# Attention and token-mixing kernel: score tiles in groups of three, one of them in two banks of the common PSUM ring

## The chip, the cores and the metric

The kernel runs on one core of one Trainium2 chip. Times are device microseconds of that core. Each time is the median of the timed runs of a kernel. All runs quoted here were fast, at a granted TensorE clock of 0.994 to 1.0. A ratio is the mean time of one kernel's fast runs over that of the other's of the same rounds, so it is not quite the ratio of the medians quoted.

The engines are called PE (TensorE), DVE (VectorE), ACT (ScalarE) and POOL (GpSimd).

## The reference

Grouped-query attention is followed by a token-mixing layer. There are 8 batches, 16 query heads on 4 key/value heads, 384 positions and a head width of 64.

```python
scores = scale * q @ k.T                       # per head, 384 x 384
attn   = softmax(scores) @ v                   # 8 x 16 x 384 x 64
x      = attn, heads side by side              # 8 x 384 x 1024
wq, wk = x @ w_q, x @ w_k                      # 1024 -> 64
mixed  = (scale * wq @ wk.T) @ x
out    = relu(mixed) @ w_out                   # 1024 x 1024
```

## The kernel before

Work is cut into 144 score tiles, 18 to a batch. One tile is 128 keys by 4 x 128 queries for two key/value heads. It takes two matmuls, one on the upper and one on the lower 64 rows of the PE array, and one exponential of 128 x 1024. PSUM has eight banks. Score tiles use `psS`, two buffers of two banks each. Everything else shares the ring `psX` of four single banks.

```python
psS = ctx.enter_context(tc.tile_pool(name="psS", bufs=2, space=PSUM))   # 2 x 2 banks
psX = ctx.enter_context(tc.tile_pool(name="psX", bufs=4, space=PSUM))   # 4 x 1 bank

def score(s, d, j, c):
    ...
    ps = psS.tile([P, 2, NH], F32, name="sc", tag="sc")
    for h in range(2):
        r = slice(D * h, D * (h + 1))                      # 64 of the 128 rows
        nc.tensor.matmul(out=ps[:, h, :], lhsT=s.kT[r, d, c, :], rhs=..., ...)

def av_task(s, d, j, h):                                   # 12 matmuls into one psX bank,
    ...                                                    # then DVE: reciprocal and multiply

def mix_banks(s, i):                                       # two psX banks, two 64-row matmuls,
    for h in range(2):                                     # each followed by a relu on DVE
        pm = psX.tile([P, S], F32, name="pmb", tag="ps")
        nc.tensor.matmul(out=pm, lhsT=s.Csb[r, ...], rhs=(s.qk if h == 0 else s.q2)[r, :], ...)
        nc.vector.tensor_relu(out=s.msb[:, ...], in_=pm)

def wout_pieces(s):                                        # the output product, as a generator:
    ...                                                    # 8 matmuls fill one psX bank ("po"),
    po = psX.tile([P, NH], F32, name="po", tag="ps")       # one per piece; between pieces the
    for n, dc in enumerate(order):                         # bank stays occupied
        nc.tensor.matmul(out=po, ...)
        ...                                                # after the 8th: copy on DVE
        yield
```

The steady loop takes two score tiles at a time. It issues both tiles' matmuls and both exponentials. Then come the tasks dealt to this group (av, projection, wk, c), with pieces of po as filler between them by a running credit. Then may come a mix.

```python
groups = [("s", steps[n:n + 2]) for n in range(0, len(steps), 2)]
...
pss = [(st, score(batches[st[0]], *st[1:])) for st in two]
for (b, d, j, c), ps in pss:
    expo(batches[b], d, j, c, ps)
...                                    # tasks and pieces
for m in mine:
    mix_step(*m)
```

## Time and profile before

| | before |
|---|---|
| time, median of 4 runs | 224.01 us |
| span of the profiled run | 221.9 us |
| PE / DVE / ACT busy | 94% / 65% / 65% |
| score visits of PE (single tiles + pairs) | 28 + 58 |
| a steady batch, from one projection to the next | 23.7 us |

The prediction below shows the lines. One habit of reading matters. PE's busy share counts a matmul from its start to its modelled end, 0.38 us for 512 columns, while such matmuls start 0.216 us apart. So a PE that waits 0.1 us between two matmuls still counts as busy, and one has to look at starts.

### The profile page before, as it was taken

What the parts mean: (1) busy time and instruction counts of PE and PEld (TensorE: products, weight loads), DVE (VectorE), ACT (ScalarE), POOL (GpSimd) and SP (SyncE); (2) the same over time, 40 slices, a digit from 0 to 9 for tenths busy, and PEclk for the clock granted to TensorE, in tenths of its full rate; (3) what the DMA queues carried; (4) which work ended last, traced back from release to release, by engine and by line L of the source; (5) the groups of instructions that cost most, each with busy time, mean ns of one, the idle gap of its engine ahead of it and who ended that gap; (6) DMA issues with size and microseconds to landing.
All of it is one profiled execution on the core that took longest, in us unless ns stands there. A gap on an engine that the chain in (4) does not pass through costs nothing.

```text
span 221.9 us, 5286 instructions
## 1 busy us (share of the span) xinstructions
PE 208.6 (94%) x2145; PEld 102.4 (46%) x2145; DVE 144.4 (65%) x371; ACT 143.6 (65%) x150; POOL 46.9 (21%) x105
## 2 busy tenths in 40 slices
PE   1899998999999999999999999999999999999992
PEld 1356554555345454554444454455445444443440
DVE  2367769757974456966687567756687578845540
ACT  2789966788688887887667777777767771001101
POOL 1499405027003220350035003400000000000000
PEclk9999999999999999999999999999999999999999
DMA  7999999999639999999999999973633231224234
GB/s 177 324 327 257 239 225 260 215 280 265 169 77 237 244 276 247 294 242 250 229 310 212 231 237 289 192 197 114 188 38 132 97 92 75 97 95 165 119 147 151
DMA packets 74574, 44.45 MB, mean 200 GB/s; under 512 B 45488, under 2 KB 70576, under 8 KB 74544
## 3 DMA queue, kind: packets, MB, share of 16 engines
q1 hardware_dynamic: 70048, 41.17, 73.0%
q0 software_dynamic: 3168, 2.36, 6.8%
q10 hardware_dynamic: 1328, 0.52, 0.9%
q8 instruction: 19, 0.31, 0.6%
q14 instruction: 11, 0.09, 0.1%
HBM read 23.59 MB, written 12.58 MB: 163 GB/s over the span
## 4 chain that ended last, share of the span: by engine, by line
PE 84%; DVE 9%; DMA 2%; ACT 2%; issue 1%; SPq 0%; ACTq 0%
PE po L276 38%; PE av L182 16%; PE sc L167 15%; PE pqk L211 5%; PE pmb L263 3%; PE pc L234 2%; DVE xnat L188 2%; DMA qraw<-in_q_dram 2%; PE ptx L196 2%; ACT pT L173 2%; DVE msb L265 2%; DVE osb L289 1%; PE ptq L154 1%; DVE qk L217 1%; PE ptw L225 1%
## 5 line engine op out<-in xcount | busy, mean ns | idle before, releaser
L173 ACT ACTIVATE pT<-sc 128x1024 bf16<-128x1024 f32 x144 | 139.7, 1022 | 41.7 <-PE sc L167 41.6
L276 PE MATMUL po<-wout_sb,msb 128*128 128x512 bf16 x384 | 102.5, 379 | 0.0
L182 PEld LDWEIGHTS <-pT 128*128 128x128 bf16 x1152 | 45.6, 98 | 17.1 <-issue 8.3
L182 PE MATMUL av<-vbf,pT 128*128 128x65 bf16 x1152 | 51.5, 195 | 0.4 <-DVE osb L289 0.3
L167 PE MATMUL sc<-qT,kT 64*128 64x512 bf16 x288 | 48.8, 391 | 1.8 <-DVE qT L159 0.8
L276 PEld LDWEIGHTS <-msb 128*128 128x128 bf16 x384 | 33.2, 97 | 35.9 <-issue 11.7
L289 DVE COPY osb<-po 128x512 f32<-128x512 f32 x46 | 31.6, 687 | 18.4 <-PE po L276 18.4
L188 DVE TENSOR_TENSOR xnat<-av,rcp_all 128x256 bf16<-128x256 f32 x96 | 40.7, 424 | 3.3
L111 POOL CAST qbf<-qraw 128x512 bf16<-128x512 f32 x46 | 26.7, 620 | 34.6 <-DMA qraw<-in_q_dram 31.9
L265 DVE TENSOR_SCALAR msb<-pmb 128x384 bf16<-128x384 f32 x56 | 28.3, 551 | 4.9 <-PE pmb L263 4.9
L187 DVE RECIPROCAL rcp_all<-av 128x4 f32<-128x4 f32 x96 | 17.1, 178 | 17.7 <-PE av L182 17.5
L167 PEld LDWEIGHTS <-kT 64*128 64x128 bf16 x288 | 13.0, 94 | 24.2 <-issue 20.3
L111 POOL CAST kbf<-kraw 128x384 bf16<-128x384 f32 x15 | 7.6, 510 | 60.1 <-DMA kraw<-in_k_dram 54.7
L252 ACT ACTIVATE msb<-pm 128x768 bf16<-128x768 f32 x2 | 1.6, 810 | 20.8 <-PE pm L246 20.8
L211 PE MATMUL pqk<-xT,wqk_sb 128*128 128x384 bf16 x64 | 11.8, 327 | 0.1
L263 PE MATMUL pmb<-qk,Csb 64*128 64x384 bf16 x28 | 9.3, 332 | 0.7 <-DVE Csb L238 0.7
L217 DVE CAST qk<-pqk 128x384 bf16<-128x384 f32 x8 | 4.5, 556 | 8.1 <-PE pqk L211 8.1
L263 PE MATMUL pmb<-q,Csb 64*128 64x384 bf16 x28 | 9.3, 331 | 0.3
L238 DVE TENSOR_SCALAR Csb<-pc 128x512 bf16<-128x512 f32 x8 | 5.5, 692 | 4.9 <-PE pc L234 4.9
L198 DVE COPY xT<-ptx 128x512 bf16<-128x512 bf16 x15 | 6.3, 421 | 3.5 <-PE ptx L196 3.5
L263 PEld LDWEIGHTS <-Csb 64*128 64x128 bf16 x56 | 3.0, 92 | 12.0 <-issue 8.8
L211 PEld LDWEIGHTS <-wqk_sb 128*128 128x128 bf16 x64 | 5.7, 97 | 5.7 <-issue 2.5
(44 smaller groups left out, 73.1 us busy)
## 6 DMA issues: line engine op xcount, KB each, us to landing
out_dram<-osb SPq DMA_DIRECT2D x23, 512.0 KB, 3.3
qraw<-in_q_dram SPq DMA_DIRECT2D x30, 384.0 KB, 5.2
kraw<-in_k_dram SPq DMA_DIRECT2D x16, 192.0 KB, 4.3
vraw<-in_v_dram SPq DMA_DIRECT2D x16, 192.0 KB, 5.2
wout_sb<-in_moe_w_out_dram POOLq DMA_DIRECT2D x4, 512.0 KB, 15.2
qraw<-in_q_dram SPq DMA_DIRECT2D x1, 512.0 KB, 5.1
qraw<-in_q_dram ACTq DMA_DIRECT2D x1, 256.0 KB, 3.8
out_dram<-osb SPq DMA_DIRECT2D x2, 128.0 KB, 2.2
```

The source lines that it names most:

```text
L111: eng.tensor_copy(out=out, in_=in_)
L167: nc.tensor.matmul(out=ps[:, h, :], lhsT=s.kT[r, d, c, :], rhs=s.qT[d][r, j, :, :].rearrange("p g n -> p (g n)"), start=True, stop=True)
L173: nc.scalar.activation(out=s.pT[d, j][:, c, :, :], in_=ps, func=AF.Exp, scale=attn_scale)
L182: nc.tensor.matmul(out=av[:, i, :], lhsT=pT[:, c, h, i * P:(i + 1) * P], rhs=s.vbf[:, g, c, :], start=(c == 0), stop=(c == C - 1))
L187: nc.vector.reciprocal(out=rcp, in_=av[:, :, D])
L188: nc.vector.tensor_tensor(out=s.xnat[:, d, j, h * G * D:(h + 1) * G * D].rearrange("p (i d) -> p i d", i=G), in0=av[:, :, :D], in1=rcp.to_ ...
L211: nc.tensor.matmul(out=s.pqk, lhsT=wqk_sb[:, dc, :], rhs=s.xT[:, dc // (DC // ND), :, dc % (DC // ND), :], start=(dc == 0), stop=(dc == DC ...
L217: nc.vector.tensor_copy(out=s.qk, in_=s.pqk)
L263: nc.tensor.matmul(out=pm, lhsT=s.Csb[r, i * P:(i + 1) * P], rhs=(s.qk if h == 0 else s.q2)[r, :], start=True, stop=True)
L265: nc.vector.tensor_relu(out=s.msb[:, h * (DC // 2) + i, :], in_=pm)
L276: nc.tensor.matmul(out=po, lhsT=s.msb[:, dc, c * P:(c + 1) * P], rhs=wout_sb[:, dc, half * NH:(half + 1) * NH], start=(n == 0), stop=(n == ...
L289: nc.vector.tensor_copy(out=osb[:, half * NH:(half + 1) * NH], in_=po)
```

## The change

The intent is to go less often into the 64-row shape of the scores. From tile 30 on, the scores of three tiles are issued together. `psS` has room for two, so the first tile of three goes to two banks of `psX`, with one exponential per bank so that each bank is freed early. At the same time the tasks are dealt out by score tile instead of by pair, and the mixes of a batch are placed beside scores, which are in the same 64-row shape.

```diff
+    def score_banks(s, d, j, c):
+        ...
+        pss = [psX.tile([P, NH], F32, name="scb", tag="ps") for h in range(2)]
+        for h in range(2):
+            nc.tensor.matmul(out=pss[h], lhsT=s.kT[r, d, c, :], ...)
+        for h in range(2):
+            nc.scalar.activation(out=s.pT[d, j][:, c, h, :], in_=pss[h], func=AF.Exp,
+                                 scale=attn_scale)
...
-        groups = [("s", steps[n:n + 2]) for n in range(0, len(steps), 2)]
+        SINGLE = 30
...                                     # at(n, ...) now by tile, not by pair
             elif b < B - 1:
-                at(g + 4, lambda b=b: proj_task(batches[b]), 1.3)
-                ...                     # wk at pair 5, c at pair 6
-                gm = (7, 8, 9, 10)      # one mix at the end of each of four pairs
+                gm = ((12, 1), (15, 0), (15, 1), (18, 0))   # (tile, 0 behind scores / 1 at the end)
+                np, nw, ncc = (6,), 9, 12
...
+        groups = [[n] for n in range(SINGLE)] + [
+            list(range(n, n + C)) for n in range(SINGLE, N + 4 * C, C)]
...
+                b, d, j, c = steps[ns[0]]
+                score_banks(batches[b], d, j, c)
+                pss = [(st, score(batches[st[0]], *st[1:])) for st in (steps[n] for n in ns[1:])]
+                for (b, d, j, c), ps in pss:
+                    expo(batches[b], d, j, c, ps)
+            for m in before:
+                mix_step(*m)
...                                     # tasks and pieces
+            for m in after:
+                mix_step(*m)
```

More of the change, by code (lines that the diff above doesn't have):

```diff
@@ L170, in score @@
         return ps
+    def score_banks(s, d, j, c):
+        if c == 0:
+            s.pT[d, j] = pt_p.tile([P, C, 2, W], BF16, name="pT", tag="pT")
+        pss = [psX.tile([P, NH], F32, name="scb", tag="ps") for h in range(2)]
+        for h in range(2):
+            r = slice(D * h, D * (h + 1))
+            nc.tensor.matmul(out=pss[h], lhsT=s.kT[r, d, c, :],
+                             rhs=s.qT[d][r, j, :, :].rearrange("p g n -> p (g n)"),
+                             start=True, stop=True)
+        for h in range(2):
+            nc.scalar.activation(out=s.pT[d, j][:, c, h, :], in_=pss[h], func=AF.Exp,
+                                 scale=attn_scale)
     def expo(s, d, j, c, ps):
@@ L338, with at @@
         per_b = ND * C * C
-        groups = [("s", steps[n:n + 2]) for n in range(0, len(steps), 2)]
+        SINGLE = 30
         todo = {}
-        def at(g, f, cost):
-            todo.setdefault(g, []).append((f, cost))
-        GB = per_b // 2
+        def at(n, f, cost=0.0, i=None):
+            t = todo.setdefault(n, [])
+            t.insert(len(t) if i is None else i, (f, cost))
         def plan(b):
-            g0 = b * GB
+            n0 = b * per_b
             def start_next():
@@ L355, in start_next @@
                         batches.append(load(b + 2))
-            at(g0, start_next, 0.0)
-            if b + 2 < B:
-                for i, g in enumerate((1, 3, 6, 8)):
-                    at(g0 + g, lambda i=i: batches[b + 2].parts[i](), 0.0)
             def casts(d, ks, vs):
@@ L374, in casts @@
                     wout_load(4 * d + 2)
+            at(n0, start_next)
+            if b + 2 < B:
+                for i, n in enumerate((2, 7, 11, 16)):
+                    at(n0 + n, lambda i=i: batches[b + 2].parts[i]())
             if b == 0:
-                at(g0, lambda: casts(0, (0,), (0,)), 0.0)
-                at(g0 + 1, lambda: casts(1, (1,), (1,)), 0.0)
-            else:
-                at(g0, lambda: casts(0, (0, 1), ()), 0.0)
-                at(g0 + 3, lambda: casts(1, (), (0, 1)), 0.0)
+                at(n0, lambda: casts(0, (0,), (0,)))
+                at(n0 + 2, lambda: casts(1, (1,), (1,)))
+            else:
+                at(n0, lambda: casts(0, (0, 1), ()))
+                at(n0 + 6, lambda: casts(1, (), (0, 1)))
@@ L381, in plan @@
                 if b + 1 < B:
-                    at(g0 + 2, lambda: kt_dma(batches[b + 1]), 0.0)
-                    at(g0 + 2, lambda: qt_dma(batches[b + 1], 0), 0.0)
-                    at(g0 + 7, lambda: qt_dma(batches[b + 1], 1), 0.0)
+                    at(n0 + 4, lambda: kt_dma(batches[b + 1]))
+                    at(n0 + 4, lambda: qt_dma(batches[b + 1], 0))
+                    at(n0 + 13, lambda: qt_dma(batches[b + 1], 1))
             for d in range(ND):
-                n0 = b * per_b + d * C * C
@@ L387, in plan @@
                 for j in range(C):
-                    g = (n0 + j * C + C - 1) // 2 + 1
+                    n = n0 + (d * C + j + 1) * C + 1
+                    end_0 = b == 0 and d == ND - 1 and j == C - 1
                     for h in range(2):
-                        at(g, lambda d=d, j=j, h=h: av_task(batches[b], d, j, h), 0.37)
+                        at(n + h - end_0, lambda d=d, j=j, h=h: av_task(batches[b], d, j, h), 0.37)
                     if b < 2 or (b == B - 1 and d == ND - 1):
-                        at(g + 1, lambda d=d, j=j: xt_task(batches[b], d, j), 0.24)
+                        soon = b < 2 and d == ND - 1 and j == C - 1
+                        at(n + (1 - end_0 if soon else 2), lambda d=d, j=j: xt_task(batches[b], d, j), 0.24)
@@ L393, in plan @@
                     elif j == C - 1:
-                        at(g, lambda d=d: xt_dma(batches[b], d), 0.0)
-                nb, nd = (b, d + 1) if d + 1 < ND else (b + 1, 0)
-                if nb < 2:
-                    g = n0 // 2 + (2 if d else 3 if b == 0 else 1)
-                    at(g, lambda nb=nb, nd=nd: kt_task(batches[nb], nd), 0.18)
-                    for j in range(C):
-                        at(g + j, lambda nb=nb, nd=nd, j=j: qt_task(batches[nb], nd, j), 0.24)
+                        at(n + 1, lambda d=d: xt_dma(batches[b], d))
@@ L403 @@
         at(0, lambda: qt_task(s0, 0, 1), 0.24)
-        at(1, lambda: qt_task(s0, 0, 2), 0.24)
+        at(2, lambda: qt_task(s0, 0, 2), 0.24)
         for b in range(B):
             plan(b)
+        for b, d, nk, nq in ((0, 1, 6, (7, 9, 12)), (1, 0, 13, (14, 17, 20)),
+                             (1, 1, 21, (22, 26, 29))):
+            at(nk, lambda b=b, d=d: kt_task(batches[b], d), 0.18)
+            for j in range(C):
+                at(nq[j], lambda b=b, d=d, j=j: qt_task(batches[b], d, j), 0.24)
@@ L426 @@
         for b in range(B):
-            g = b * GB + GB
-            if b < 2:
-                at(g + 1, lambda b=b: proj_task(batches[b], 0), 0.65)
-                at(g + 1, lambda b=b: proj_task(batches[b], 1), 0.65)
-                todo.setdefault(g + 2, []).insert(1, (lambda b=b: wk_task(batches[b]), 0.17))
-                at(g + 2, lambda b=b: c_task(batches[b]), 0.75)
-                gm = (3, 3, 4, 4)
+            n = (b + 1) * per_b
+            if b == 0:
+                gm = ((6, 0), (7, 0), (8, 0), (9, 0))
+                np, nw, ncc = (2, 3), 4, 5
+            elif b == 1:
+                gm = ((6, 1), (9, 0), (9, 1), (12, 0))
+                np, nw, ncc = (3, 3), 5, 6
             elif b < B - 1:
-                at(g + 4, lambda b=b: proj_task(batches[b]), 1.3)
-                todo.setdefault(g + 5, []).insert(0, (lambda b=b: wk_task(batches[b]), 0.17))
-                todo.setdefault(g + 6, []).insert(0, (lambda b=b: c_task(batches[b]), 0.75))
-                gm = (7, 8, 9, 10)
-            else:
-                at(g + 2, lambda b=b: proj_task(batches[b]), 1.3)
-                at(g + 3, lambda b=b: wk_task(batches[b]), 0.17)
-                at(g + 4, lambda b=b: c_task(batches[b]), 0.75)
-            if b < B - 1:
-                for i in range(DC // 2):
-                    mixes.setdefault(g + gm[i], []).append((b, i))
+                gm = ((12, 1), (15, 0), (15, 1), (18, 0))
+                np, nw, ncc = (6,), 9, 12
+            else:
+                gm = ()
+                np, nw, ncc = (5,), 6, 9
+            for i, m in enumerate(np):
+                part = i if len(np) > 1 else None
+                at(n + m, lambda b=b, part=part: proj_task(batches[b], part), 1.3 / len(np))
+            at(n + nw, lambda b=b: wk_task(batches[b]), 0.17, (1, None)[b] if b < 2 else 0)
+            at(n + ncc, lambda b=b: c_task(batches[b]), 0.75, 0 if b else None)
+            for i, (m, e) in enumerate(gm):
+                mixes.setdefault((n + m, e), []).append((b, i))
         oki = m_p.tile([P, 1], I32, name="oki", tag="oki")
@@ L467, in count @@
             nc.vector.tensor_copy(out=oki[:1, :], in_=pok[:1, :])
-        PIECE, MIX, LEAN, KEEP = 0.218, 0.2, 1.54, 12
+        PIECE, MIX, LEAN, KEEP = 0.218, 0.2, 0.77, 12
         per_piece = C * (Dm // NH) * DC
-        g0 = (B // 2) * GB
-        even = (sum(c for g in range(g0, g0 + GB) for f, c in todo.get(g, []))
-                + (DC // 2) * MIX + per_piece * PIECE) / GB
-        ramp = 4 * GB + 2
-        end = (B - 1) * GB + GB + 2
-        credit = 0.0
-        def tile_of(st):
-            b, d, j, c = st
-            expo(batches[b], d, j, c, score(batches[b], d, j, c))
@@ L484 @@
-        for g in range(end + 3):
-            two = groups[g][1] if g < len(groups) else []
-            tasks = todo.get(g, [])
-            mine = mixes.get(g, [])
-            credit += (LEAN if g < ramp else even) - sum(c for f, c in tasks) - MIX * len(mine)
+        mid = range(B // 2 * per_b, (B // 2 + 1) * per_b)
+        even = (sum(c for n in mid for f, c in todo.get(n, []))
+                + (DC // 2) * MIX + per_piece * PIECE) / per_b
+        ramp = 4 * per_b + 3
+        N = len(steps)
@@ new lines, with mix_step @@
+        at(N + 4, lambda: ok.append(range_test()))
+        at(N + 8, lambda: count(ok[0]))
+        ok = []
+        groups = [[n] for n in range(SINGLE)] + [
+            list(range(n, n + C)) for n in range(SINGLE, N + 4 * C, C)]
+        credit = 0.0
+        def mix_step(b, i):
+            mix_banks(batches[b], i)
+            if i == DC // 2 - 1:
+                filler.append(wout_pieces(batches[b]))
+                left[0] += per_piece
+        for ns in groups:
+            before, after = ([m for n in ns for m in mixes.get((n, e), [])] for e in range(2))
+            tasks = [t for n in ns for t in todo.get(n, [])]
+            credit += (LEAN if ns[0] < ramp else even) * len(ns)
+            credit -= sum(c for f, c in tasks) + MIX * len(before + after)
@@ L489 @@
             n = min(max(0, int(credit / PIECE)), left[0])
-            if g >= end:
-                more = sum(per_piece for b, i in mine if i == DC // 2 - 1)
-                n = min(left[0], (left[0] + more - KEEP) // (end + 3 - g))
+            if ns[0] >= N + C:
+                more = sum(per_piece for b, i in before + after if i == DC // 2 - 1)
+                n = min(left[0], (left[0] + more - KEEP) // ((N + 4 * C - ns[0]) // C))
             credit = min(credit - n * PIECE, 0.5)
-            ops = []
@@ L496 @@
-            for i, t in enumerate(tasks):
-                ops.append(t)
-                ops += [(piece, PIECE)] * (n * (i + 1) // len(tasks) - n * i // len(tasks))
-            if not tasks:
-                ops = [(piece, PIECE)] * n
-            def mix_step(b, i):
-                mix_banks(batches[b], i)
-                if i == DC // 2 - 1:
-                    filler.append(wout_pieces(batches[b]))
-                    left[0] += per_piece
-            if g < GB + 5 and two:
-                tile_of(two[0])
-                if len(mine) == 2:
-                    mix_step(*mine.pop(0))
-                half, run = sum(c for f, c in ops) / 2, 0.0
-                while ops and run + ops[0][1] / 2 <= half:
-                    run += ops[0][1]
-                    ops.pop(0)[0]()
-                tile_of(two[1])
-            else:
-                pss = [(st, score(batches[st[0]], *st[1:])) for st in two]
+            if len(ns) == 1:
+                b, d, j, c = steps[ns[0]]
+                expo(batches[b], d, j, c, score(batches[b], d, j, c))
+            elif ns[0] < N:
+                b, d, j, c = steps[ns[0]]
+                score_banks(batches[b], d, j, c)
+                pss = [(st, score(batches[st[0]], *st[1:])) for st in (steps[n] for n in ns[1:])]
@@ L520 @@
                 for (b, d, j, c), ps in pss:
                     expo(batches[b], d, j, c, ps)
-                if len(mine) == 2:
-                    mix_step(*mine.pop(0))
-            for f, c in ops:
-                f()
-            if g == end - 1:
-                ok = range_test()
-            if g == end + 1:
-                count(ok)
-            for m in mine:
+            for m in before:
+                mix_step(*m)
+            for i, (f, c) in enumerate(tasks or [(lambda: None, 0.0)]):
+                f()
+                of = max(1, len(tasks))
+                for _ in range(n * (i + 1) // of - n * i // of):
+                    piece()
```

## The prediction

> **What bounds the kernel now.** I read the page's busy table and chain first, then busy time by stretch, then the order of instructions in a steady and in an unsteady stretch.
>
> ```profile
> PE 208.6 (94%) x2145; PEld 102.4 (46%) x2145; DVE 144.4 (65%) x371; ACT 143.6 (65%) x150; POOL 46.9 (21%) x105
> ...
> PE 84%; DVE 9%; DMA 2%; ACT 2%; issue 1%; SPq 0%; ACTq 0%
> ```
>
> TensorE (PE) is the bound: 84% of the chain of waits. By stretch (busy us of 25, with counts; the granted clock is 1.00 in all):
>
> ```profile
> 10.00:35.00 25.00, 23.48 (x312) 14.28 (x311) 16.98 (x51) 21.41 (x23) 14.73 (x28) 1.00 1.20 262
> ...
> 60.00:85.00 25.00, 24.68 (x276) 11.94 (x274) 14.70 (x41) 20.89 (x23) 5.39 (x12) 1.00 0.89 201
> ...
> 110.00:135.00 25.00, 25.00 (x263) 11.48 (x260) 17.66 (x44) 18.15 (x20) 5.75 (x13) 1.00 1.00 246
> 135.00:160.00 25.00, 25.00 (x282) 12.22 (x281) 17.82 (x46) 18.74 (x20) 4.52 (x11) 1.00 0.77 198
> ```
>
> From 85 us on PE never idles; VectorE (DVE, third pair) and ScalarE (ACT, fourth) have 25% or more to spare. Before that there are gaps, and ACT is the next-fullest. But busy is not streaming, so I looked at starts:
>
> ```profile
> 120.88 0.59 PE L276 MATMUL po<-wout_sb,msb 128*128 128x512 bf16 x2
> 121.41 0.60 PE L167 MATMUL sc<-qT,kT 64*128 64x512 bf16 x4
> 121.94 0.61 PE L276 MATMUL po<-wout_sb,msb 128*128 128x512 bf16 x2
> ```
>
> Two po matmuls span 0.59 us and one lasts 0.38, so they start 0.215 us apart. The second starts at 121.10 and should hand over at 121.31; the score starts at 121.41. Four score matmuls are two concurrent pairs (each half uses 64 of the array's rows): 2 x 0.216 = 0.43, yet the next po starts 0.53 after them. So each excursion into the 64-row shape loses 0.094 us going in and 0.092 coming out. The second pair starts 7 ns late and the second po 11 ns late: 0.20 us per visit. Summing starts over 100 to 175 us, these changes of shape are practically the only loss, about 20 changes and 1.9 us in each 25 us. The steady state has no wait for a buffer at all. In the first 85 us there are, besides the changes, about 10 us of waits, 4 of them in the first 10 us while inputs arrive.
>
> The third thing to see is a place where the common PSUM ring (psX, four banks) is already short:
>
> ```profile
> 57.83 0.38 PE L276 MATMUL po<-wout_sb,msb 128*128 128x512 bf16 x1
> 58.14 0.33 PE L263 MATMUL pmb<-qk,Csb 64*128 64x384 bf16 x1
> 58.47 0.33 PE L263 MATMUL pmb<-q,Csb 64*128 64x384 bf16 x1
> 58.48 0.76 PE L167 MATMUL sc<-qT,kT 64*128 64x512 bf16 x4
> 59.02 0.33 PE L263 MATMUL pmb<-qk,Csb 64*128 64x384 bf16 x1
> 59.48 0.32 PE L263 MATMUL pmb<-q,Csb 64*128 64x384 bf16 x1
> ```
>
> ```profile
> 58.33 0.17 DVE L187 RECIPROCAL rcp_all<-av 128x4 f32<-128x4 f32 x1
> 58.54 0.42 DVE L188 TENSOR_TENSOR xnat<-av,rcp_all 128x256 bf16<-128x256 f32 x1
> 58.88 1.94 DVE L265 TENSOR_SCALAR msb<-pmb 128x384 bf16<-128x384 f32 x4
> ```
>
> This is mix, two scores, mix. The two halves of a mix should start together, 3 ns apart. The second mix's halves start 0.46 us apart. A po accumulation, eight matmuls dealt out one by one, holds the fourth bank, so only three rotate. Four mix halves need four: the last waits until the relu of the first half, 58.88 + 0.55 = 59.43, has freed one, and starts 0.05 later. Both mixes together lose about 0.6 us.
>
> **What the Trainium skill says.** "TensorEngine Tiling (Array Packing)", Key Properties: "Changing tiling mode (not just tile) drains the TensorE". The trace agrees, at 0.09 us a change. "PSUM — Partial Sum Buffer", Engine vs sequencer instructions: matmuls start and complete in program order. So a score waiting for a bank also holds everything behind it; at 59.48 above the po matmuls wait behind the mix. "ScalarE: Activation LUTs", What ACT_TABLE_LOAD costs: an ACTIVATE with immediate scale and bias takes 186 ns + 0.833 ns an element. That gives 1039 ns for 1024 columns, and the trace has 1022, so my estimate for a 512-column one is about 0.61 us. The page has back-to-back ones overlap by 93 ns; the trace has two in 1.94 us, an overlap of about 0.1.
>
> **The change part by part.**
>
> Removed shape changes. Before, the first 28 tiles go singly and 116 in 58 pairs: 86 visits. After, 30 singly and 114 in 38 triples: 68. A lone mix at the end also joins another. I walked the task order of both versions on paper, arithmetic of the credits included, and get 185 changes of shape before and 147 after (19 and 13 per steady batch). The walk's order for before is the order in the trace. 38 x 0.094 + 19 x 0.018 = 3.9 us, all on the path.
>
> Added exponentials. One 1022 ns ACTIVATE becomes two of about 0.61 us: 0.1 us more per triple, 4 us in all, on an engine with slack. A triple needs about 3.0 us of ACT. A lean triple (PE 3 x 0.77 of dealt work, 3 x 0.22 of scores, 0.2 of changes) takes about 3.15, so this just fits and I charge nothing.
>
> Added demand on the ring. Each triple takes two psX banks. With plain av tasks this is harmless: ACT frees the two at about 1.05 and 1.6 us after the scores start, and the task that needs them comes later. Two places in a steady batch are not harmless. First, mixes: of the four per batch, two pairs now stand as mix, banked score, two scores, mix. In my walk a po is half done at every one of these. Three rotating banks then serve the mix's two halves and the score's first half; the score's second half must wait for the mix's first relu. Counted from that mix half: 0.33 matmul, 0.04 latency, 0.55 relu, 0.05 semaphore = 0.98 us, against 0.17 where it would have started. Loss 0.81 us, and PE works in order, so all of it is on the path. Batches 1 to 6 have two such clusters each; in the last there is no score but two mixes in a row, which costs about 0.7. In batch 1 the mix comes right behind two av and a po copy, with DVE 0.7 us behind: about 1.6. Sum 10 x 0.81 + 1.6 + 0.7 = 10.4 us. Second, the projection group (proj, av, av and a few po, then scores): DVE must do two 0.56 us casts of pqk before the first av's 0.6 us, so its bank is free about 0.35 us after the banked score wants it, in five batches: 1.7 us. Together +12 us.
>
> Dealing by tile. In the first 30 tiles each tile gets at most two tasks or so; wk and c move one tile behind the projection; the four mixes of batch 0 are spread over four tiles. Before, the waits around those mixes (33 to 39 us) sum to some 2.4 us. An estimate of 1.5 us gained, perhaps 3 of the 6 us of waits between 10 and 85 us. The last 35 us stay as they are: PE streams po there whatever the order.
>
> Sum: 224.0 - 3.9 - 1.5 + 12 = 230.6 us.
>
> **Rivals.** (1) The ring does not bite: the schedule behaves as the change intends and only changes of shape go away, 224.0 - 3.9 - 1.5 = 218.6, up to 217 with a better ramp. For it: the steady trace before has no buffer wait, DVE is at 70%, and the placing of the mixes beside the scores looks deliberate. Against it: the 58 to 59.5 us stretch shows just this shortage with one bank less in demand. (2) ACT becomes the bound in the lean stretch (60 to 85 us, already 20.89 of 25): a late exponential holds a score bank and the saving of batches 2 and 3 is lost; 220 to 222 without ring waits. Only a few 0.15 to 0.2 us waits between score pairs there speak for it. (3) Ring waits and a much better ramp cancel: 4 to 5 us out of the first 85 us, giving 224 to 228.
>
> **Range and chances.** The ring argument is arithmetic with measured durations, and I trust its sign; but a detailed schedule like this was probably kept because it ran no worse, so I move the point from 230.6 towards rival 3: 228.0. The range runs from just inside rival 1 to a DVE somewhat further behind than I reckoned: 219.5 to 232.5. Chances: faster 0.12, same 0.41, slower 0.47.
>
> **What would show it.** Right: between 85 and 180 us PE shows starts of the second bank of a score 0.5 us or more after the first, next to mixes, released by the relu; a steady batch lasts about 25 us (before 23.7 in the chain, from one projection to the next); about 150 shape changes. Wrong: a steady batch of about 23.1 us, with the pmb and the banked scores starting in pairs 3 ns apart, means rival 1. ACT above 95% busy between 45 and 85 us with scores waiting for exponentials means rival 2. A first 85 us shorter by over 4 us means rival 3.

## The result

The changed kernel takes 234.09 us (233.94 to 234.63, 4 runs) against 224.01 us (223.74 to 224.29). The ratio is 1.0454, with a 95% interval of 1.0433 to 1.0475. It is slower by 10 us and lies 1.6 us above the top of the predicted range.

The busy table and the chain of the changed kernel's page:

```profile
PE 210.1 (91%) x2113; PEld 105.7 (46%) x2145; DVE 145.4 (63%) x371; ACT 145.2 (63%) x188; POOL 47.0 (20%) x105
...
PE 77%; DVE 12%; DMA 4%; ACT 3%; issue 2%; SPq 0%; ACTq 0%
```

PE is still the bound, but its part of the chain fell from 84% to 77% and DVE's rose from 9% to 12%. PE does the same work, so DVE now releases PE at more places. (The profile has 2113 of 2145 matmul records; the 32 missing are all po.)

Busy time of the engines in the same stretches as before:

```profile
10.00:35.00 25.00, 23.19 (x291) 13.18 (x291) 16.31 (x48) 21.35 (x23) 14.74 (x28) 1.00 1.20 262
...
60.00:85.00 25.00, 22.70 (x261) 11.74 (x263) 16.31 (x44) 19.77 (x27) 5.39 (x12) 1.00 0.71 186
...
110.00:135.00 25.00, 24.07 (x250) 11.99 (x254) 16.87 (x43) 17.78 (x25) 5.39 (x12) 1.00 0.95 236
135.00:160.00 25.00, 23.75 (x252) 11.96 (x255) 16.65 (x43) 17.78 (x25) 4.95 (x11) 1.00 0.75 198
```

In the steady stretches PE now has visible gaps of about 1 us in each 25. There no engine is fuller than before: from 110 to 135 us ACT went from 18.15 to 17.78, DVE from 17.66 to 16.87. So nothing became a bound by its amount of work, and the gaps must be waits for something in particular. The order of PE instructions around a mix shows it:

```profile
114.63 0.59 PE L290 MATMUL po<-wout_sb,msb 128*128 128x512 bf16 x2
115.16 0.33 PE L277 MATMUL pmb<-qk,Csb 64*128 64x384 bf16 x1
115.16 0.33 PE L277 MATMUL pmb<-q,Csb 64*128 64x384 bf16 x1
115.53 0.39 PE L179 MATMUL scb<-qT,kT 64*128 64x512 bf16 x1
116.14 0.37 PE L179 MATMUL scb<-qT,kT 64*128 64x512 bf16 x1 [0.22 <-DVE msb L279]
116.14 0.80 PE L167 MATMUL sc<-qT,kT 64*128 64x512 bf16 x4
116.66 0.32 PE L277 MATMUL pmb<-qk,Csb 64*128 64x384 bf16 x1
116.78 0.32 PE L277 MATMUL pmb<-q,Csb 64*128 64x384 bf16 x1
```

and what DVE did meanwhile:

```profile
114.83 0.18 DVE L201 RECIPROCAL rcp_all<-av 128x4 f32<-128x4 f32 x1
115.05 0.42 DVE L202 TENSOR_TENSOR xnat<-av,rcp_all 128x256 bf16<-128x256 f32 x1
115.53 1.02 DVE L279 TENSOR_SCALAR msb<-pmb 128x384 bf16<-128x384 f32 x2
```

The first half of the banked score (scb) should follow the mix (pmb) after 0.17 us. It starts at 115.53, when the av's multiply (ending at 115.47) has freed a bank. The second half should start with the first. It starts 0.61 us later, at 116.14, when the first relu (115.53 + 0.55) has freed another, 0.98 us after the mix. The square bracket names that relu. It says only 0.22 us because PE counts as idle only after the modelled end of the last matmul.

I summed such delays over the whole program. For each run of 64-row matmuls and each run of others, I took the time from its first start to the start of the next run, less the spacing that its matmuls have when nothing waits (0.216 us for 512 columns, 0.163 for 384, 0.033 for an av matmul, 0.056 for a transpose, half for concurrent pairs) and less 0.094 for the change of shape. The missing po records were filled in from the program's order. Microseconds:

| PE loses on | before | after |
|---|---|---|
| changes into and out of the 64-row shape, 176 and 138 at 0.094 | 16.5 | 13.0 |
| waits in the first 50 us | 10.5 | 11.9 |
| later: around mixes | 2.5 | 11.8 |
| later: other score visits | 1.3 | 3.6 |
| later: the rest | 1.4 | 2.4 |
| sum | 32.2 | 42.7 |

The difference of 10.5 us agrees with that of the spans, 232.2 - 221.9 = 10.3. The steady batch went from 23.7 to 25.1 us. Not all of the last four rows is waiting: the c product (pc) has a third shape, 128 rows by 64 columns, and nine of its changes of shape in each kernel, at about 0.09 us, stand in these rows. With them the traces have exactly the 185 and 147 changes that the prediction counted on paper.

### The profile page after: what moved, and what is told of

Its sections match the earlier page's. It is cut to its first block, busy times and chain, and to the rows that moved or that the text cites. A ratio compares the mean times of both kernels' runs of the same rounds, so it can differ in the third digit from the quotient of the medians.

```text
span 232.2 us, 5293 instructions
## 1 busy us (share of the span) xinstructions
PE 210.1 (91%) x2113; PEld 105.7 (46%) x2145; DVE 145.4 (63%) x371; ACT 145.2 (63%) x188; POOL 47.0 (20%) x105
## 4 chain that ended last, share of the span: by engine, by line
PE 77%; DVE 12%; DMA 4%; ACT 3%; issue 2%; SPq 0%; ACTq 0%
PE po L290 33%; PE av L196 15%; PE sc L167 9%; PE scb L179 6%; PE pqk L225 4%; DVE xnat L202 4%; DVE msb L279 4%; PE pc L248 3%; PE ptx L210 2%; DMA qraw<-in_q_dram 2%; PE pmb L277 2%; DMA xT<-xnat 2%; ACT pT L183 2%; DVE rcp_all L201 1%; PE ptq L154 1%
## 5 line engine op out<-in xcount | busy, mean ns | idle before, releaser
L187 ACT ACTIVATE pT<-sc 128x1024 bf16<-128x1024 f32 x106 | 103.5, 1031 | 10.5 <-PE sc L167 10.2
L290 PE MATMUL po<-wout_sb,msb 128*128 128x512 bf16 x352 | 95.5, 379 | 1.4 <-issue 0.2
L183 ACT ACTIVATE pT<-scb 128x512 bf16<-128x512 f32 x76 | 42.0, 595 | 39.7 <-PE scb L179 39.0
L196 PEld LDWEIGHTS <-pT 128*128 128x128 bf16 x1152 | 47.5, 98 | 20.6 <-issue 5.2
L196 PE MATMUL av<-vbf,pT 128*128 128x65 bf16 x1152 | 52.3, 195 | 0.8 <-issue 0.2
L290 PEld LDWEIGHTS <-msb 128*128 128x128 bf16 x384 | 31.7, 97 | 30.6 <-issue 9.1
L167 PE MATMUL sc<-qT,kT 64*128 64x512 bf16 x212 | 40.5, 396 | 0.9 <-DVE qT L159 0.5
L179 PE MATMUL scb<-qT,kT 64*128 64x512 bf16 x76 | 22.4, 383 | 5.8 <-DVE msb L279 2.6
L167 PEld LDWEIGHTS <-kT 64*128 64x128 bf16 x212 | 11.1, 94 | 16.5 <-issue 10.3
L179 PEld LDWEIGHTS <-kT 64*128 64x128 bf16 x76 | 4.5, 93 | 17.6 <-DVE xnat L202 8.0
```

Of the source, the lines that this page charges most:

```text
L179: nc.tensor.matmul(out=pss[h], lhsT=s.kT[r, d, c, :], rhs=s.qT[d][r, j, :, :].rearrange("p g n -> p (g n)"), start=True, stop=True)
L183: nc.scalar.activation(out=s.pT[d, j][:, c, h, :], in_=pss[h], func=AF.Exp, scale=attn_scale)
L187: nc.scalar.activation(out=s.pT[d, j][:, c, :, :], in_=ps, func=AF.Exp, scale=attn_scale)
L196: nc.tensor.matmul(out=av[:, i, :], lhsT=pT[:, c, h, i * P:(i + 1) * P], rhs=s.vbf[:, g, c, :], start=(c == 0), stop=(c == C - 1))
L290: nc.tensor.matmul(out=po, lhsT=s.msb[:, dc, c * P:(c + 1) * P], rhs=wout_sb[:, dc, half * NH:(half + 1) * NH], start=(n == 0), stop=(n == ...
```

## The experiments

Theory A: the ring of four banks is short. A score tile in two of its banks, mixes on both sides of it and a half-done po make PE wait for DVE or ACT to free a bank. Rival B: the new dealing of the work by tile is to blame. Rival C: the halved exponentials are. I ran twelve kernels; each was also run beside the kernel before on the same chip, at 224.2 to 224.7 us. All twelve outputs passed, even that of the one which leaves work out.

### Pairs in place of triples

The triples of the changed kernel become pairs in `psS`; everything else stays.

```diff
-            list(range(n, n + C)) for n in range(SINGLE, N + 4 * C, C)]
+            [n, n + 1] for n in range(SINGLE, N, 2)] + [list(range(n, n + C)) for n in range(N, N + 4 * C, C)]
...
-                score_banks(batches[b], d, j, c)
-                pss = [... for st in (steps[n] for n in ns[1:])]
+                pss = [... for st in (steps[n] for n in ns)]
```

> The changed kernel with its steady triples replaced by pairs in the two score banks; the dealing of the work by tile stays. My theory: the loss is PE waiting for banks of the common ring because a score tile takes two of them, above all beside the mixes (11.8 us summed over the changed kernel's trace) and in other triples (5 us). Without banked scores that goes: 185 changes of shape as before, a second mix half still waits some 0.3 us in six places, so 224 to 227 us. Rival, the new dealing of the work by tile costs the time: it stays over 230 us.

Measured: 231.16 us, ratio 1.0284 (1.0254 to 1.0314). This is a miss. Of the 10 us only 3 to 4 went away with the banked tile, and as it stands the result favours B. The trace shows two losses that I had not reckoned. The first is in the list of waits (engine, operation, what released it, us in total, times, longest):

```profile
PE pqk L225 <- DMA xT<-xnat: 3.4, 3, 1.8
```

In three batches the projection waits for the transposing DMA, because in pairs "tile 6" comes earlier in program order than in triples or in the kernel before. (The kernel before has no such wait; the changed kernel has one of 0.36 us, in batch 2.) The second: the close-set mixes lose 0.6 to 0.7 us in each of six batches even with nothing banked.

### Mixes away from the scores

```diff
-                gm = ((12, 1), (15, 0), (15, 1), (18, 0))
+                gm = (16, 17, 19, 20)          # as tasks, each behind an av (shortened)
```

> The changed kernel, with the mixes of batches 1 to 6 put behind the av tasks, away from the scores; triples, banked scores and dealing stay. My theory: the waits next to mixes (11.8 us) go, and 46 more changes of shape cost 46 x 0.094 + 23 x 0.018 = 4.7 us, so about 227 us (226 to 229). Rivals (the halved exponentials, or the dealing by tile): the extra changes of shape come on top and the time is 234 to 239 us.

Measured: 234.35 us, ratio 1.0436 (1.041 to 1.0463). This is a miss as well: no gain. By the same sums the waits around mixes fell from 11.8 to 2.8 us, as A says. But the 46 added changes of shape cost 4.3 us, and other waits grew: triples without a mix from 5.0 to 8.4 us over the whole program, the rest from 7.8 to 9.1. My reading is that a mix in the middle of a triple takes two turns of the same ring, and a later score pays; no run tests that by itself.

### The banked tile last

```diff
-                score_banks(...) ; score ; score
+                score ; score ; score_banks(...)        # exponentials: 1st, the two halves, 2nd
```

> The changed kernel, with the banked score tile third instead of first on PE, and its two exponentials between the two others on ACT. My theory: the banked halves are wanted 0.43 us later, so each of twelve waits beside a mix shrinks from 0.81 to about 0.4 us (5 us less) and most of the 5 us of waits in other triples goes (3 to 4 us less); av waits for the later exponentials may give back 1 to 2 us. 225 to 228 us. Rivals: the number of instructions of each kind is the same, so about 234 us.

Measured: 241.47 us, ratio 1.0747 (1.0714 to 1.0781). The sign is wrong. PE around a mix in this kernel:

```profile
118.04 0.33 PE L275 MATMUL pmb<-qk,Csb 64*128 64x384 bf16 x1
118.05 0.33 PE L275 MATMUL pmb<-q,Csb 64*128 64x384 bf16 x1
118.22 0.59 PE L167 MATMUL sc<-qT,kT 64*128 64x512 bf16 x4
118.65 0.75 PE L179 MATMUL scb<-qT,kT 64*128 64x512 bf16 x2
119.49 0.32 PE L275 MATMUL pmb<-qk,Csb 64*128 64x384 bf16 x1
120.26 0.32 PE L275 MATMUL pmb<-q,Csb 64*128 64x384 bf16 x1 [0.45 <-ACT pT L524]
```

The banked halves (two matmuls in 0.75 us) lose less, as expected. The second mix now waits, until 120.26, for the banks of the banked tile, whose exponentials stand later in ACT's order. The list of waits has a mix released by a halved exponential 11 times, for 4.8 us of idle time. The place lost 0.81 us before and loses 1.40 now. That contradicts B and C, which expected no difference, but it also shows that my estimate had followed one wait and not the next user of the bank.

### Halved exponentials in the kernel before

```diff
-                    expo(batches[b], d, j, c, ps)          # first tile of each steady pair
+                    for h in range(2):
+                        nc.scalar.activation(out=pT[:, c, h, :], in_=ps[:, h, :], func=AF.Exp, ...)
```

> The kernel before, with the first exponential of every steady pair cut into two of 512 columns. It adds 58 ACT instructions, about 6 us of ACT, more than the change adds (38). My theory: ACT has slack and the time stays 224.0 within 0.7 us. Rival, the halved exponentials are what costs: 224 + 10 x 58/38, about 239 us, or some part of it.

Measured: 225.00 us, ratio 1.0014 (0.999 to 1.0037). Rival C is out. A halved exponential takes 0.595 us in the changed kernel, against 1.022 for a whole one in the kernel before, and ACT has room for it.

### Banked tiles in the kernel before

The second tile of each steady pair goes to two `psX` banks with halved exponentials, in the old order. Nothing is saved and nothing dealt anew.

```diff
-                pss = [(st, score(...)) for st in two]
+                ps = score(... two[0]) ; scb = [psX.tile(...), psX.tile(...)] ; matmuls of two[1]
+                expo(ps) ; two halved exponentials of scb
```

> The kernel before in its own order, with the second tile of each steady pair in two banks of the common ring and its exponential halved: no change of shape is saved and nothing is dealt anew. My theory: demand on the ring alone costs. A mix at the end of a group holds two of three free banks, so the banked tile's second half waits until 0.98 us after the mix instead of 0.39, some three times a batch, and av tasks wait for the late exponentials: 1.8 to 3.5 us a batch, 233 to 245 us. Rival, the dealing by tile is the cause: 224 to 226 us.

Measured: 255.38 us, ratio 1.1383 (1.1338 to 1.1428). Taking banks of the ring costs 31 us with nothing else changed but the halving of exponentials, which the last run cleared. That is above my range. PE behind a mix in this kernel:

```profile
134.16 0.33 PE L263 MATMUL pmb<-q,Csb 64*128 64x384 bf16 x1
134.33 0.38 PE L167 MATMUL sc<-qT,kT 64*128 64x512 bf16 x2
134.55 0.38 PE L528 MATMUL scb<-qT,kT 64*128 64x512 bf16 x1
135.14 0.37 PE L528 MATMUL scb<-qT,kT 64*128 64x512 bf16 x1 [0.22 <-DVE msb L265]
```

The second half starts 0.98 us after the mix, as reckoned, and the 21 visits with a mix and a banked tile lose 16.1 us together. What I undersized is the other part: runs of av, po and other tasks went from 6.2 to 21.8 us of waits, and the list of waits has av released by a halved exponential 14 times, for 6.1 us of idle time. The halves come after the first tile's whole exponential on ACT, so av could be waiting for their banks or for their results. The two traces settle it. From 44 us on, 21 av here start after PE has idled for over 0.15 us. In the kernel before, where they have the same place in the program, the same 21 start 0.8 to 1.8 us after their scores, and each before the last exponential of that pair has ended. So they do not use that result, and what they wait for here is a bank.

### Pairs with the old places

As the first experiment, with projection and mixes of batches 2 to 6 where the kernel before has them.

```diff
-                gm = ((12, 1), (15, 0), (15, 1), (18, 0)) ; np, nw, ncc = (6,), 9, 12
+                gm = ((14, 1), (16, 1), (18, 1), (20, 1)) ; np, nw, ncc = (8,), 10, 12
```

> As e1 (dealt by tile, pairs, nothing banked), with projection and mixes of batches 2 to 6 put back to where the kernel before has them. In e1's trace the projection waited 0.5 to 1.9 us for the transposing DMA in three batches and the close-set mixes cost 0.7 us in each of six. If those two are the whole of e1's 6.4 us, as I now think, this gives 224 to 227 us. Rival, dealing by tile costs by itself: it stays near 231 us.

Measured: 225.27 us, ratio 1.0035 (0.9995 to 1.0076). Dealing by tile costs at most 0.8% by the interval, which includes no cost at all. Rival B is out as far as dealing by itself goes. The *places* given to projection and mixes are another matter.

### Pairs with close-set mixes

As the last one, with only the mixes put back to the places of the changed kernel.

```diff
-                gm = ((14, 1), (16, 1), (18, 1), (20, 1))
+                gm = ((12, 1), (15, 0), (15, 1), (18, 0))
```

> As e7 (pairs, dealt by tile, projection in its old place), with the mixes of batches 2 to 6 in the places of the changed kernel, one before and one behind the scores of a group. It tells the two differences between e1 (231.2 us) and e7 (225.3 us) apart. In e1's trace a close-set pair of mixes lost 0.6 to 0.7 us in each of six batches although nothing was banked. If that holds, five more such places give 225.3 + 3.5 = 228 to 230 us. If e1's loss was all the projection waiting for the transposing DMA, 225 to 226 us.

Measured: 228.40 us, ratio 1.0160 (1.0117 to 1.0204). So the close-set mixes cost about 3 us with nothing banked, and the rest of the first experiment's loss, 231.16 - 228.40 = 2.8 us, goes with the earlier projection.

### Every tile alone

```diff
-        SINGLE = 30
+        SINGLE = 144
```

(with the old places for projection and mixes)

> As e7 (dealt by tile, old places of projection and mixes), with every score tile alone instead of in pairs: 295 changes of shape instead of 187, so 54 more visits. If a visit costs the 0.20 us read from the starts, 54 x 0.20 = 11 us more than e7's 225.3: 235 to 238 us. If the changes are hidden behind something else, 226 to 230 us.

Measured: 236.22 us, ratio 1.0535 (1.0507 to 1.0563). That is 10.95 us over the pairs with old places, for 54 more visits: 0.203 us a visit. The price of a visit, read from starts in one profile, holds.

### The banked tile left out

Its output is wrong, which doesn't matter for the time. Triples, dealing, mixes and visits stay, and only the tile that used `psX` is not computed.

```diff
-                score_banks(batches[b], d, j, c)
+                batches[b].pT[d, j] = pt_p.tile(...) ; left_out.add((b, d, j))
...                                     # av reads the second tile's exponentials in its place
```

> The changed kernel with the banked tile of every triple left out (the result is wrong on purpose; av reads the second tile's exponentials in its place). Visits, dealing, mixes and all other work stay; 38 x 0.216 = 8.2 us of score matmuls go. My theory: the two banks are what made PE wait, so some 16 us of waits go too and about 5 us stay (a second mix half 0.4 us late in twelve places): 234.3 - 8 - 11 = 215 us (213 to 218). Rival, the grouping in threes or the dealing is the cause: 226 us, the 8 us alone.

Measured: 219.71 us, ratio 0.9794 (0.976 to 0.9828). The kernel is 14.4 us shorter than the changed one. 38 tiles at 0.216 us are 8.2 us of work, so 6.2 us of waits went: less than A's 11 and more than B's 0. (The edit takes the tile's exponentials from ACT as well, 38 us of its busy time; so it removes more than the two banks.) By the same sums the waits around mixes fell by 4.9 us and those of other triples by some 4, but runs of other tasks lost some 2.5 us more. What is left around a mix:

```profile
109.13 0.33 PE L280 MATMUL pmb<-qk,Csb 64*128 64x384 bf16 x1
109.14 0.33 PE L280 MATMUL pmb<-q,Csb 64*128 64x384 bf16 x1
109.31 0.59 PE L167 MATMUL sc<-qT,kT 64*128 64x512 bf16 x4
109.74 0.32 PE L280 MATMUL pmb<-qk,Csb 64*128 64x384 bf16 x1
110.12 0.32 PE L280 MATMUL pmb<-q,Csb 64*128 64x384 bf16 x1
```

Two mixes, one on each side of the scores, take four banks, and three rotate. The last half waits until 0.98 us after the first mix, just as the banked score did. Waits around mixes still come to 6.9 us in this kernel (11.8 in the changed one), and the projection, now earlier, waits 2.2 us for the transposing DMA. So the waits around mixes have two causes that overlap: without the banked tile 6.9 of 11.8 us stay, and with the mixes set apart (second experiment) 2.8 stay. The bank that one of them would find free the other has taken.

### The po in one go

All eight matmuls of a po stand behind the first av, so that no po is half done across scores and four banks rotate.

```diff
-                for _ in range(n * (i + 1) // of - n * i // of):
+                for _ in range(8 if f in first_av and credit_left else 0):      # shortened
                     piece()
```

> The changed kernel, with the eight matmuls of a po issued in one go behind the first av of a triple, so that no half-done po holds a bank across scores: four banks rotate instead of three. Mixes stay beside the scores. My theory: the waits of triples without a mix (5 us) mostly go; beside a mix the second half then waits for the av before the mix (0.7 us instead of 0.8), so only 1 us goes there. 229 to 232 us. Rivals (halved exponentials, dealing): 234 to 235 us.

Measured: 234.40 us, ratio 1.0461 (1.0406 to 1.0515). No gain. Triples without a mix lost 2.2 us instead of 5.0 over the whole program. But next to a mix the banked tile then waits for the po's copy and the av, 1.03 us instead of 0.81 to 0.97, and the projection came too early for the transposing DMA in places. A fourth bank that DVE has just begun to empty is not a free bank.

### The po in one go and the mixes in the middle

```diff
+                    if f in first_av:
+                        for m in mid_mix:
+                            mix_step(*m)                   # then the eight matmuls of a po
```

> As e8, and one mix a triple, between the first av and the po. Triples, banked scores, halved exponentials and the dealing by tile all stay; 46 changes of shape are added (4.7 us). My theory: by the bank order (scores 1 and 2, av 3, mix 4 and 1, po 2, av 3, next scores 4 and 1) nothing waits in the steady state, so 16 us of waits go: 224 to 227 us. Rivals: 238 to 240 us, from the added changes of shape.

Measured: 235.21 us, ratio 1.049 (1.0448 to 1.0532). The bank order was right where I had worked it out. PE in a steady triple with a mix:

```profile
118.44 0.39 PE L179 MATMUL scb<-qT,kT 64*128 64x512 bf16 x2
118.66 0.59 PE L167 MATMUL sc<-qT,kT 64*128 64x512 bf16 x4
119.19 0.55 PE L196 MATMUL av<-vbf,pT 128*128 128x65 bf16 x12
119.67 0.33 PE L277 MATMUL pmb<-qk,Csb 64*128 64x384 bf16 x1
119.68 0.33 PE L277 MATMUL pmb<-q,Csb 64*128 64x384 bf16 x1
```

Two banked halves fit into 0.39 us and two mix halves start together. Nothing waits there. But the 46 changes of shape cost their 4.3 us, and I had not worked out the other triples. The mix behind a projection lost 0.65 us in four batches. Triples without a po are shorter than their exponentials, and some wait 1.1 us for ACT. After the last score the program runs 2.6 us longer than the kernel before, some 1.6 of it in waits. All waits fell from 29.7 only to 25.7 us.

### One ring of eight banks

All scores are in single banks of one ring of eight, with one mix behind the scores of a triple, and each po inside a triple.

```diff
-    psS = ... bufs=2 ; psX = ... bufs=4
+    psX = ... bufs=8                   # every score half its own bank and its own exponential
```

> An attempt at a version that beats both: triples, but all eight PSUM banks in one ring, every exponential per bank, one mix a triple right behind the scores, and each po begun and ended inside a triple. 151 changes of shape. If banks are the limit and eight in one ring turn over fast enough, a steady batch takes about 23.5 us and the first 50 us stay as in the changed kernel: 223 to 228 us. If the six banks that a triple then takes at once are too many, 230 us and more.

Measured: 226.92 us, ratio 1.0129 (1.0111 to 1.0148). This is the best of the kernels with full triples, 7 us better than the changed one and still slower than the kernel before. PE has no gap from 110 to 160 us. Waits around mixes fell to 7.3 us after the first 50 us. About half of those left stand between 50 and 100 us, where the triples have least other work. The edit moves mixes and po as well as the banks, so the 7 us can't be put down to the ring alone. No variant beat the kernel before.

## Why the prediction was wrong

**What bounds the kernel, and the price of a visit: right.** The experiment with single tiles gives 0.203 us for the predicted 0.20. The trace has 38 fewer changes of shape, 3.6 us at 0.094, for the predicted 3.9.

**Ring demand beside mixes: right in kind and nearly in size.** Predicted was a loss of 0.81 us at each of ten places, 1.6 at one and 0.7 at the last, 10.4 in all. Measured were 0.81 to 1.29, 1.69 and 1.03, 11.8 in all, and 9.3 net of the 2.5 that the kernel before lost there, which the prediction did not subtract. The 0.98 us from a mix to the reuse of its bank appears in four different kernels. What the prediction put down to the banked half alone is only half its doing. Without the banked tile the mixes still lose 6.9 us, and with pairs they cost 3 us. The prediction had reckoned this loss for the second mix nowhere in the changed kernel, where it hides behind the first. So the mechanism was right, and that the size came out so near is partly luck.

**Projection group: 1.7 us predicted, 2.5 measured** (0.69, 0.35, 0.35, 0.57, 0.57). Other visits add another 1.1 us, 0.55 of it in a triple of batch 2 right behind wk.

**Dealing by tile: the term of the sum that failed.** The prediction booked 1.5 us of gain in the first 30 tiles. The waits in the first 50 us went from 10.5 to 11.9 us instead. Of these, 1.4 us are the first three banked triples, for which the prediction had charged nothing; without them 10.5 are left, as before. With pairs the same dealing took 0.8 us more, within noise of nothing. So the gain did not come, and this term alone is off by 2.9 us. The reading under it was off too: the prediction saw "about 10 us of waits" in the first 85 us, where the later sums give 13.

**Exponentials: right.** Halving 58 of them in the kernel before changed the time by 0.14%.

**Range and chances: the second step that failed.** The working summed to 230.6 us, 3.5 us short of the 234.09 measured. Then the prediction says "a detailed schedule like this was probably kept because it ran no worse, so I move the point from 230.6 towards rival 3". Nothing in the profile supports that sentence. It took 2.6 us off the point, and with it stand a range that ends at 232.5 and only 0.47 for slower. Without it, the missing 3.5 us are the ramp term (2.9), 0.6 at the projection and other visits (2.3 net for 1.7), 0.3 at the changes of shape and 1.0 in the rest, less 1.1 at the mixes; these roundings sum to 3.7. The three rivals were all false, and their own tests said so: scores do not start in pairs next to mixes, a batch takes 25.1 us and not 23.1, ACT is busy 19.77 of 25 us between 60 and 85 us, and the first 85 us did not get shorter. (One more reading was off without harm: of the kernel before the prediction says that ACT has 25% or more to spare from 85 us on, but from 85 to 110 us it is busy 20.20 of 25. And the place at 58 us lost 0.74 us by the same sums, for its 0.6.)

**What stays open.** The shares of banked tile and close-set mixes can't be added up exactly, since each wait has both as causes. No run gave the ring of the changed kernel one more bank with all else equal: `psS` and `psX` already take all eight. And the repairs that I tried were each mis-predicted for one reason: I worked out the place that I wanted to mend and not where the next user of the bank would stand.

## What to carry to other kernels

A saving on the bound engine is worth nothing if it is paid for with buffers that this engine then waits for: count the banks wanted within one turnover (here 0.98 us, matmul and relu) before moving a tile into a shared ring. When a shared ring is short, work through every user in order, because here a wait that was removed reappeared at the next. And once a sum is worked out from measured durations, do not shade it with a guess about why somebody made the change.

## What the Trainium skill lacked or had wrong

- "TensorEngine Tiling (Array Packing)", Key Properties, says that changing the tiling mode drains TensorE, and gives no size. Here a change costs 0.092 to 0.094 us and a visit to the 64-row shape 0.20 us; 54 added visits cost 10.95 us.
- "PSUM — Partial Sum Buffer", Summary: rules for kernel authors, says to evacuate promptly and gives no turnover time. Here a bank could be written again 0.98 us after the start of a 384-column matmul followed by a relu on an idle DVE (0.33 matmul, 0.04, 0.55 relu, 0.05), and three rotating banks with four users inside that time cost 0.4 to 0.8 us each time.
- "Perfetto Trace Analysis", Summary: the profiler window per engine type, says that a TensorE instruction's end is estimated, and not what follows for waits. Here the profile showed 0.22 us of idle time where a start came 0.61 us late, because the modelled end covers the rest; the starts of the matmuls carried the whole argument.
- "ScalarE: Activation LUTs", What ACT_TABLE_LOAD costs: 186 ns + 0.833 ns an element gives 1039 and 613 ns for 1024 and 512 columns. The means are 1022 in the kernel before, 1031 and 595 in the changed one, 1 to 3% less. But in the run with one ring the 212 half exponentials of the other tiles (sc) have a mean of 664 and a median of 632, more than the page gives.
